# Preparing an expert's weight sums: adding transfers in place of GpSimd sums, and signs moved into activations and shares

## The chip, the cores and the metric

The kernel runs on one core of a Trainium2 chip. The metric is the device time of one execution in microseconds. Three executions of the kernel before took 1699.41, 1706.53 and 1699.93 us; their median is 1699.93 us.

The engines are named as in the profile: PE is TensorE with its matmuls (PEld its weight loads), DVE is VectorE, ACT is ScalarE, POOL is GpSimd, and SP is SyncE, which issues nearly all transfers.

## The reference

Three layers follow each other. First an attention (2 batches, 8 heads, 768 positions, 64 wide) in which a query sees only the keys that have the same nearest centroid. Its output, 1536 tokens of 512, goes through a feed-forward layer, and then through 8 experts whose shares come from a balanced gate:

```python
h = x @ w_in                                  # 512 -> 2048
g = np.maximum(h, 0.0) + np.log1p(np.exp(-np.abs(h)))
x = g @ w_out                                 # 2048 -> 512

P = np.exp(x @ w_gate - max)                  # 1536 x 8, then 8 rounds of
                                              # normalizing rows and columns
for e in range(8):
    h = np.maximum(x @ w1[e], 0.0)            # 512 -> 1024
    out += P[:, e:e+1] * (h @ w2[e])          # 1024 -> 512
```

## The kernel before, in words

**The work and its stages.** Everything is float32, and a float32 product is made of three matmuls on a high and a low part of each operand. So each operand is split: ACT makes the high part, DVE or POOL subtracts it from the original for the low part. The attention takes the first 315 us, the feed-forward layer runs from 315 to about 612 us, the experts from 636 us to the end. The expert stage does 16 passes (2 batches times 8 experts), `NB` of them with index `k`; its first layer is `l1_group` (L899 is its matmul), its second `l2_piece` (L934).

**Seven products in place of eight.** Each expert product is cut into 2 x 2 blocks, and both layers use a scheme of seven block products with sums of blocks on both sides (`PROD`). On the side of the activations the sums are S1 to S4 (`SUMS`): A21 + A22, S1 - A11, A11 - A21, A12 - S2. They are made on the fly by `g_sum` (L872, DVE), `x_sums` (L72) and `xc_prep` (L973). On the side of the weights the sums are T1 to T4, which depend on the weights alone: B12 - B11, B22 - T1, B22 - B12 and T2 - B21. Each is needed twice (once for each batch), so they are made once, in advance, and stored to the DRAM tensors `TD`. From there the expert stage loads them like the blocks that need no sum: `w1_load` (L801, L806, L813, L817) into `wf` and `w1r`, and `w2_load` (L849, L851) into `w2r`.

**Making the sums before the change.** A unit of this work is one tile `ts` of 128 x 4 x 256: a piece of each of the four blocks of one weight matrix. `JOBS` lists 64 units, four for each of 16 matrices. `t_load` (L195) loads the pieces with two transfers from SP, `t_sums` (L201) makes the four sums in place with four subtractions on POOL, `t_store` (L206, L211) writes them to `TD` from SP:

```python
b11, b12, b21, b22 = (t[:, n, :] for n in range(4))
for o_, u_, v_ in ((b11, b12, b11), (b12, b22, b12), (b22, b22, b11), (b21, b21, b22)):
    nc.gpsimd.tensor_tensor(o_, u_, v_, ALU.subtract)
```

Sixteen units (two experts' matrices) are planned into the attention, 24 into the feed-forward layer, 24 into the expert stage. Tiles `ts` have 3, 4 and 1 buffers in the three stages.

**What sets the order.** The attention is a list of events with a step each (`at`), written out in that order. The feed-forward layer goes over 16 blocks of work (`m1`), each with seven places `i`; `tsum_at` puts the sums' parts at such places, a new unit every 3.9 of them. The expert stage is a list of calls with a time (`do`), sorted by it; a time unit is one group of first-layer products, a pass has `G1` = 28 of them, and a new unit of sums comes every 7. The time of a call is its place in the program; the order on each engine and each queue is then made by a scheduler that may put an instruction forward where its operands allow it. On the chip each engine and each queue works strictly in its order, so an instruction that waits holds up whatever is behind it.

**What else is on POOL.** In the feed-forward layer POOL makes low parts of the weights (L243, L247) and of x (L100). In the expert stage it makes the low parts of the second layer's weights, vl (L857), and of a part of the first layer's, wlCm (L829). In the attention it splits q, k and v (L355, L356, L49, L372) and does parts of the choice of centroids (L416, L424). The feed-forward layer's weights are 64-bit words, which DVE turns into float32 (`to32`, L118 to L121) ahead of the splits; its activation ends on DVE with gf (L660), whose low part is L663.

Of the kernel before, what the change touches and what calls it, by code (L numbers as in the profile page):

```python
# [7 lines left out]
F32 = mybir.dt.float32  # L8
# [3 lines left out]
AF = mybir.ActivationFunctionType  # L12
# [8 lines left out]
def attention_moe_moe2(ctx, tc, v, qt, kt, centroids, w_in, w_out, w_gate, w1, w2, eye, out, dbg=None):  # L21
# [39 lines left out]
    def x_blocks(x):  # L61
# [1 line left out]
        return {f"A{i + 1}{j + 1}": x[:, j * hk : (j + 1) * hk, i * h2 : (i + 1) * h2] for i in range(2) for j in range(2)}  # L63

    SUMS = {
        "S1": ("A21", "A22", ALU.add), "S2": ("S1", "A11", ALU.subtract),
        "S3": ("A11", "A21", ALU.subtract), "S4": ("A12", "S2", ALU.subtract),
    }

    def x_sum(blk, name, t, eng):  # L70
        u, v, op = SUMS[name]
        eng.tensor_tensor(t, blk[u], blk[v], op)  # L72
        blk[name] = t

    def x_sums(key, x):
# [103 lines left out]
        [tc.dram_tile([4, NF2, P, DM // 2], F32, name=f"td1_{e}") for e in range(E)],  # L179
    ]  # L180
    TS = {}
    TORD = ("T1", "T3", "T4", "T2")

    def t_load(pool, m, e, u):
        t = TS[m, e, u] = slot_pool[pool].tile([P, 4, 256], F32, tag="ts", name=f"ts{m}_{e}_{u}", bufs=TSB[pool])
        for h in range(2):
            if m:
                o = h * HF + u * P
                src, d = w2[e, o : o + P, :].rearrange("p (s d) -> p s d", s=2), t[:, 2 * h : 2 * h + 2, :]
            else:  # L190
                k, c = divmod(u, 2)
                o = h * DM // 2 + k * P
                src = w1[e, o : o + P, :].rearrange("p (s f) -> p s f", s=2)[:, :, c * 256 : (c + 1) * 256]
                d = t[:, 2 * h : 2 * h + 2, :]
            nc.sync.dma_start(d, src)  # L195

    def t_sums(m, e, u):
        t = TS[m, e, u]
        b11, b12, b21, b22 = (t[:, n, :] for n in range(4))
        for o_, u_, v_ in ((b11, b12, b11), (b12, b22, b12), (b22, b22, b11), (b21, b21, b22)):  # L200
            nc.gpsimd.tensor_tensor(o_, u_, v_, ALU.subtract)  # L201

    def t_store(m, e, u):
        t = TS.pop((m, e, u))
        if m:
            nc.sync.dma_start(TD[1][e][:, u].rearrange("s p d -> p s d"), t)  # L206
            return
        k, c = divmod(u, 2)
        cs = slice(c * 256, (c + 1) * 256)
        for n, ts_ in enumerate((t[:, 0:4:3, :], t[:, 1:3, :])):  # L210
            nc.sync.dma_start(TD[0][e][2 * n : 2 * n + 2, k, :, cs].rearrange("s p f -> p s f"), ts_)  # L211

    TSB = {"ap": 3, "fp": 4, "gp": 1}
    JOBS = [(m, e, u) for e in range(E) for m in range(2) for u in range(NF2)]
    JA, JF = 4 * NF2, 10 * NF2

    WT = {}

# [103 lines left out]
    def at(step, fn, cat=None):  # L322
        events.append((step, len(events), fn, cat))
# [266 lines left out]
        at(92 + (n - 1) * 1.36, lambda n=n: fetch_first(n), ("fu", 0))  # L590
    for n in range(4):
        at(175 + n * 5, lambda n=n: x_split("1_0", first_blk, n), ("xs", 0))
    for n, job in enumerate(JOBS[:JA]):
        t = 22 + 10 * n
        for o, fn, c_ in ((0, t_load, "tl"), (8, t_sums, "tq"), (17, t_store, "tw")):
            at(t + o, lambda fn=fn, job=job: fn(*((("ap",) if fn is t_load else ()) + job)), (c_, 0))
    KEEP = {'sp2': 1, 'fr': 0, 'av': 1, 'am3': 1, 'tpa': 1, 'smc': 0, 'm0': 1, 'rw': 1, 'pz': 1, 'e1': 1}
    events.sort(key=lambda x: x[:2])
    last_prep = max(key for key, _, fn, _ in events if fn in prep_fns)
# [100 lines left out]
    nc.gpsimd.memset(ones_f, 1.0)  # L700
    lt = mp.tile([P, B * NT, E], F32, tag="lt", name="lt", bufs=1)
    Pt = mp.tile([P, B * NT, E], F32, tag="Pt", name="Pt", bufs=1)

    def gtile(shape, tag, b, nm):
        return ps_y.tile(shape, F32, tag=tag, name=nm) if b else ps_l.tile(shape, F32, tag="lb", name=nm)
# [33 lines left out]
    def sinkhorn(it, ph):  # L739
        n = B * NT  # L740
        if ph == 0:
            rs = mp.tile([P, n], F32, tag="rs", name=f"rs{it}", bufs=1)
            nc.vector.tensor_reduce(rs, Pt, AX.X, ALU.add)
            nc.vector.tensor_scalar(rs, rs, 1e-9, None, ALU.add)
            nc.vector.reciprocal(rs, rs)
            nc.vector.tensor_tensor(Pt, Pt, rs.unsqueeze(2).to_broadcast([P, n, E]), ALU.mult)
            cs = G["cs"] = mp.tile([P, E], F32, tag="cs2", name=f"cs{it}", bufs=1)
            nc.vector.tensor_reduce(cs, Pt.rearrange("p t e -> p e t"), AX.X, ALU.add)
            return
        cs = G["cs"]  # L750
        cp = ps_y.tile([P, E], F32, tag=f"y{2 + it % 2}", name=f"cp{it}")
        nc.tensor.matmul(cp, ones_f, cs, start=True, stop=True)
        nc.vector.tensor_scalar(cs, cp, 1e-9, float(E) / N, ALU.add, ALU.mult)
        nc.vector.reciprocal(cs, cs)
        nc.vector.tensor_tensor(Pt, Pt, cs.unsqueeze(1).to_broadcast([P, n, E]), ALU.mult)

    def run(*steps):
        for l in steps:
# [105 lines left out]
        return t  # L864

    def g_sum(k, name, p):
        u_, v_, op = SUMS[name]
        if name in ("S1", "S2"):
            t = x_tile(k, name, p)
        else:  # L870
            t = XG[k, name, p] = XG[k, {"S3": "A21", "S4": "A12"}[name], p]
        nc.vector.tensor_tensor(t, XG[k, u_, p], XG[k, v_, p], op)  # L872

    def g_split(k, i, p):
        src = XG[k, PROD[i][0], p]
# [7 lines left out]
    def l1_group(k, u, i):  # L883
# [33 lines left out]
            else:  # L917
                nc.vector.tensor_tensor(t[:, v], ps, LB["c", {1: 0, 4: 3, 5: 2}[i]], ALU.add)  # L918
        if v and i != 6:
            nc.scalar.activation(t, t, AF.Relu)  # L920

    def l2_piece(k, i, p, t):
        sb, e = divmod(k, E)
# [19 lines left out]
        for t_ in ((0, 1) if t == 1 else (2,)):  # L943
            m = r * HT + t_
            src = y[t_ // 2][:, t_ % 2 * 256 : t_ % 2 * 256 + 256]
            acc = yv[:, m, c * 256 : (c + 1) * 256]
            scl = Pt[:, sb * NT + m, e : e + 1]
            with tc.high_priority(30):
                if e == 0 and i in (0, 2, 3, 6):
                    nc.vector.tensor_scalar(acc, src, scl, None, ALU.mult)  # L950
                else:
                    nc.vector.scalar_tensor_tensor(acc, src, scl, acc, ALU.mult, ALU.add)  # L952
            if e == E - 1 and i in (5, 6):
                nc.sync.dma_start(out.rearrange("(b p t) d -> b t p d", b=B, t=NT)[sb, m], yv[:, m])

    def xc_prep(sb, step):
# [7 lines left out]
            ]  # L964

        def add(name):
            a, b, op = SUMS[name]
            if name == "S4":
                t = blk["S2"]
            else:  # L970
                tag = {"S1": "A22", "S2": "A12", "S3": "A21"}[name]
                t = gp.tile([P, 2, FH], F32, tag="X" + tag, name=f"x{name}{key}", bufs=XB[tag])
            nc.vector.tensor_tensor(t, blk[a], blk[b], op)  # L973
            blk[name] = t

        def split(name):
# [17 lines left out]
    for k in range(NB):  # L994
# [26 lines left out]
        for j in range(14):  # L1021
# [2 lines left out]
            do(first[j] + 0.1, g_split, k, i, p)  # L1024
            for n in range(3):
                do(S0 + lag + sp * j + sp * n / 3 + 0.01, l2_piece, k, i, p, n)
    for n, job in enumerate(JOBS[JF:]):
        t = G1 + 7 * n + 1.5
        do(t, t_load, "gp", *job)
        do(t + 3, t_sums, *job)  # L1030
        do(t + 5.5, t_store, *job)
    for hf in range(2):
        do(0.5 + hf, lambda hf=hf: gate(1, hf))
        do(2.5 + 1.5 * hf, lambda hf=hf: gate_max(hf))
# [2 lines left out]
            do(5.5 + 4 * it + 2.5 * ph, lambda it=it, ph=ph: sinkhorn(it, ph))  # L1037

    tsum_at = {}
    for n, job in enumerate(JOBS[JA:JF]):  # L1040
        for o, fn in ((0, lambda job=job: t_load("fp", *job)), (5, lambda job=job: t_sums(*job)),
                      (10, lambda job=job: t_store(*job))):
            tsum_at.setdefault(divmod(int(3.9 * n) + o, 7), []).append(fn)

    for n, u in enumerate(m1):
        if dbg is not None and n == dbg.get("cut"):
# [75 lines left out]
```

## Time and profile before

| | us |
|---|---|
| median of three executions | 1699.93 |
| the profiled execution | 1703.77 |
| its span, from the first to the last instruction | 1702.0 |
| PE busy | 1552.5 (91%) |
| DVE busy | 1277.2 (75%) |
| ACT busy | 1007.3 (59%) |
| POOL busy | 852.2 (50%) |
| POOL busy with the weights' sums (L201, 256 instructions) | 228.0 |

The page gives an average over stages that have different limits. To read it, one goes from the slices to the windows: a stretch in which PE runs its matmuls back to back at a granted clock of 1.00 gives the rate of that stage, and the stretches that fall short of it are those where something can be gained or lost.

### The profile page before, as it was taken

What the parts mean: (1) busy time and instruction counts of PE and PEld (TensorE: products, weight loads), DVE (VectorE), ACT (ScalarE), POOL (GpSimd) and SP (SyncE); (2) the same over time, 40 slices, a digit from 0 to 9 for tenths busy, and PEclk for the clock granted to TensorE, in tenths of its full rate; (3) what the DMA queues carried; (4) which work ended last, traced back from release to release, by engine and by line L of the source; (5) the groups of instructions that cost most, each with busy time, mean ns of one, the idle gap of its engine ahead of it and who ended that gap; (6) DMA issues with size and microseconds to landing.
All of it is one profiled execution on the core that took longest, in us unless ns stands there. A gap on an engine that the chain in (4) does not pass through costs nothing. (4 is left out here: it accounts for less than half of the span.)

```text
span 1702.0 us, 27339 instructions
## 1 busy us (share of the span) xinstructions
PE 1552.5 (91%) x9873; PEld 1474.4 (87%) x9873; DVE 1277.2 (75%) x1835; ACT 1007.3 (59%) x1854; POOL 852.2 (50%) x728
## 2 busy tenths in 40 slices
PE   5898888798799998888788999998999999999998
PEld 4787877687799977887778999998999999999998
DVE  4988878896666366966565788789788787878877
ACT  4777777654465544554454665665565666656664
POOL 3443545676611125666666454456445455444554
PEclk7998999899999999999998999999999999999999
DMA  7657663467622005555555444433443444334422
GB/s 217 175 157 193 173 176 120 131 229 248 209 75 75 22 26 164 177 183 167 179 178 173 127 121 119 127 117 94 148 129 119 127 124 124 114 115 125 122 78 75
DMA packets 265464, 236.27 MB, mean 139 GB/s; under 512 B 13296, under 2 KB 244848, under 8 KB 265328
## 3 DMA queue, kind: packets, MB, share of 16 engines
q1 hardware_dynamic: 265184, 234.46, 45.6%
q8 instruction: 77, 1.26, 0.3%
q14 instruction: 59, 0.48, 0.1%
q10 hardware_dynamic: 144, 0.07, 0.0%
HBM read 177.32 MB, written 36.70 MB: 126 GB/s over the span
## 5 line engine op out<-in xcount | busy, mean ns | idle before, releaser
L857 POOL TENSOR_TENSOR vl<-w2r,vh 128x512 fp32r<-128x512 f32 x224 | 354.3, 1584 | 373.4 <-ACT vh L856 339.6
L201 POOL TENSOR_TENSOR ts<-ts 128x256 f32<-128x256 f32 x256 | 228.0, 894 | 123.5 <-DMA ts<-in_moe_w_dram 109.7
L878 DVE TENSOR_TENSOR gl<-XA,gh 128x768 fp32r<-128x768 f32 x160 | 172.9, 1082 | 86.7 <-ACT gh L877 86.5
L877 ACT CAST gh<-XA 128x768 fp32r<-128x768 f32 x160 | 133.9, 837 | 148.5 <-PE Ya1m L934 134.8
L934 PE MATMUL Ya0m<-vl,gh 128*128 128x256 f32 x512 | 145.9, 285 | 0.0
L934 PE MATMUL Ya0m<-vh,gl 128*128 128x256 f32 x512 | 145.9, 285 | 0.0
L934 PE MATMUL Ya0m<-vh,gh 128*128 128x256 f32 x512 | 145.9, 285 | 0.0
L856 ACT CAST vh<-w2r 128x512 fp32r<-128x512 f32 x224 | 137.6, 615 | 11.0 <-PE y L680 8.2
L536 DVE TENSOR_TENSOR el<-t,eh 128x384 fp32r<-128x384 f32 x192 | 102.6, 549 | 21.8 <-ACT eh L532 20.3
L934 PE MATMUL Yb0m<-vl,gh 128*128 128x256 f32 x384 | 109.4, 285 | 4.0 <-POOL vl L857 4.0
L934 PE MATMUL Yb0m<-vh,gl 128*128 128x256 f32 x384 | 109.6, 285 | 2.1 <-DVE gl L878 2.1
L934 PE MATMUL Yb0m<-vh,gh 128*128 128x256 f32 x384 | 109.3, 285 | 2.3 <-DVE x L952 2.3
L497 DVE TENSOR_REDUCE sc<-s 128x1 f32<-128x768 f32 x96 | 91.1, 950 | 25.9 <-PE s L489 25.6
L532 ACT CAST eh<-t 128x384 fp32r<-128x384 f32 x192 | 91.1, 481 | 29.0 <-PE t L529 19.5
L529 PE MATMUL t<-idf,E 128*128 128x128 f32 x576 | 100.3, 284 | 5.3 <-ACT OHT L437 2.8
L920 ACT ACTIVATE XA<-XA 128x768 f32<-128x768 f32 x96 | 81.1, 845 | 34.5 <-DVE XA L918 34.5
L502 ACT ACTIVATE E<-s,sc 128x768 f32<-128x768 f32 x96 | 87.1, 907 | 20.4 <-DVE sc L497 19.3
L934 PEld LDWEIGHTS Ya0m<-vh,gl 128*128 128x128 f32 x512 | 98.9, 193 | 0.0
L934 PEld LDWEIGHTS Ya0m<-vh,gh 128*128 128x128 f32 x512 | 98.9, 193 | 0.0
L934 PEld LDWEIGHTS Ya0m<-vl,gh 128*128 128x128 f32 x512 | 98.8, 193 | 0.0
L529 PEld LDWEIGHTS t<-idf,E 128*128 128x128 f32 x576 | 75.0, 146 | 16.0 <-DVE el L536 5.2
L877 ACT CAST gh<-XS 128x768 fp32r<-128x768 f32 x64 | 53.4, 836 | 58.4 <-PE Yb1m L934 44.2
(243 smaller groups left out, 5355.0 us busy)
## 6 DMA issues: line engine op xcount, KB each, us to landing
ts<-in_moe_w_dram SPq DMA_DIRECT2D x128, 256.0 KB, 4.0
w2r<-td SPq DMA_DIRECT2D x64, 512.0 KB, 4.0
w2r<-in_moe_w_dram SPq DMA_DIRECT2D x48, 512.0 KB, 3.6
td<-ts SPq DMA_DIRECT2D x64, 256.0 KB, 3.7
td<-ts SPq DMA_DIRECT2D x32, 512.0 KB, 3.3
wf<-td SPq DMA_DIRECT2D x64, 256.0 KB, 3.1
w1r<-td SPq DMA_DIRECT2D x64, 256.0 KB, 3.1
AT<-HL SPq DMA_DIRECT2D x64, 192.0 KB, 3.9
```

Source lines behind the costliest of these rows:

```text
L201: nc.gpsimd.tensor_tensor(o_, u_, v_, ALU.subtract)
L497: nc.vector.tensor_reduce(SC[i][:, 0, j, t : t + 1], Et[i, t][:, :, 0:CB], AX.XY, ALU.max, negate=True)
L502: nc.scalar.activation(e.rearrange("p (a c) -> p a c", a=2), Et[i, t][:, :, 0:CB], AF.Exp, bias=sc[:, 0, j, t : t + 1], scale=1.0, accum_o ...
L529: nc.tensor.transpose(pt[:, t * P : (t + 1) * P], Et[i, t][:, s * P : (s + 1) * P], idf)
L532: nc.scalar.copy(eh, TT[i, s])
L536: nc.vector.tensor_tensor(el, TT.pop((i, s)), EHL[i, s].bitcast(F32), ALU.subtract)
L856: nc.scalar.copy(h, src)
L857: nc.gpsimd.tensor_tensor(l, src, h.bitcast(F32), ALU.subtract)
L877: nc.scalar.copy(h, src)
L878: nc.vector.tensor_tensor(l, src, h.bitcast(F32), ALU.subtract)
L920: nc.scalar.activation(t, t, AF.Relu)
L934: nc.tensor.matmul(ps, g[:, v, ts], w[:, v, :], start=i in (0, 1, 3) and p == 0 and v == 0 and n == 0 and t != 1, stop=p == 1 and v == 1 a ...
```

## The change

Each weight matrix is now one chain of ten steps on one tile of 128 x 1024, a whole block at a time. Three kinds of steps: a plain load of a block (SP), a load that adds a block to what the tile holds (issued by POOL, `accum_op=ALU.add`), and a store of the tile to `TD` (SP). `STEPS` lists them: load B11, add B12, store T1, add B22, store T2, add B21, store T4, load B12, add B22, store T3. There are 16 chains in place of 64 units: 4 in the attention, 6 in the feed-forward layer, 6 in the expert stage, with 1, 2 and 1 tiles. Each step is bound behind the last PE instruction written before it (`behind_pe`), which holds it at its place in the schedule; it adds no wait on the chip. The steps come 4.1 steps apart in the attention, 2.85 places apart in the feed-forward layer (two chains side by side) and 2.75 time units apart in the expert stage.

So that all of these sums are additions, some blocks and sums change their sign. On the activations' side S1 = A22 - A21, S2 = -S1 - A11, S3 = A11 - A21 and S4 = -S2 - A12, of which S2 and S4 become scalar_tensor_tensor instructions. The first layer's activations take Relu with a scale of -1 where the block comes out negated (all but A11 and A21), and the second layer's right half is added with `Nt`, the negated shares, in place of `Pt`.

```diff
     SUMS = {
-        "S1": ("A21", "A22", ALU.add), "S2": ("S1", "A11", ALU.subtract),
-        "S3": ("A11", "A21", ALU.subtract), "S4": ("A12", "S2", ALU.subtract),
+        "S1": ("A22", "A21", 1.0, ALU.subtract), "S2": ("S1", "A11", -1.0, ALU.subtract),
+        "S3": ("A11", "A21", 1.0, ALU.subtract), "S4": ("S2", "A12", -1.0, ALU.subtract),
     }
+    def sum_op(eng, out_, a, b, sign, op):
+        if sign > 0:
+            eng.tensor_tensor(out_, a, b, op)
+        else:
+            eng.scalar_tensor_tensor(out_, a, sign, b, ALU.mult, op)
...
-    TORD = ("T1", "T3", "T4", "T2")
...
+    TORD = ("T1", "T2", "T3", "T4")
+    STEPS = ("B11", "+B12", "T1", "+B22", "T2", "+B21", "T4", "B12", "+B22", "T3")
+
+    def t_step(pool, m, e, n):
+        what = STEPS[n]
+        if n == 0:
+            TS[m, e] = slot_pool[pool].tile([P, 1024], F32, tag="ts", name=f"ts{m}_{e}", bufs=TSB[pool])
+        t, w = TS[m, e], what.lstrip("+")
+        t = t.rearrange("p (k f) -> p k f", k=NF2 if m else 2)
+        if w[0] == "T":
+            nc.sync.dma_start(TD[m][e][TORD.index(w)].rearrange("k p f -> p k f"), t)
+            return
...
+        src = src.rearrange("(k p) f -> p k f", p=P)
+        if what[0] == "+":
+            nc.gpsimd.dma_start(t, src, accum_op=ALU.add)
+        else:
+            nc.sync.dma_start(t, src)
+
+    def behind_pe(fn, *args):
+        traced = nc.cur_bb.bb.instructions
+        ref, last = next(iter(last_of_engines(("PE",)))), traced[-1]
+        fn(*args)
+        start = next(n for n in reversed(range(len(traced))) if traced[n] is last) + 1
+        for ins in list(traced[start:]):
+            tc.add_manual_dep(
+                ins, ref.name,
+                mybir.DependencyInfo(mybir.DependencyClass.NoSync, mybir.DependencyReason.DATA), reason="order",
+            )
...
-    TSB = {"ap": 3, "fp": 4, "gp": 1}
-    JOBS = [(m, e, u) for e in range(E) for m in range(2) for u in range(NF2)]
-    JA, JF = 4 * NF2, 10 * NF2
+    TSB = {"ap": 1, "fp": 2, "gp": 1}
+    JOBS = [(m, e) for e in range(E) for m in range(2)]
+    JA, JF = 4, 10
...
-    for n, job in enumerate(JOBS[:JA]):
-        t = 22 + 10 * n
-        for o, fn, c_ in ((0, t_load, "tl"), (8, t_sums, "tq"), (17, t_store, "tw")):
-            at(t + o, lambda fn=fn, job=job: fn(*((("ap",) if fn is t_load else ()) + job)), (c_, 0))
+    for j, job in enumerate(JOBS[:JA]):
+        for n in range(10):
+            at(22 + 42 * j + 4.1 * n, lambda job=job, n=n: behind_pe(t_step, "ap", *job, n), ("tl", 0))
...
+        if it == 7:
+            nc.vector.tensor_scalar(Nt, Pt, -1.0, None, ALU.mult)
...
-            nc.scalar.activation(t, t, AF.Relu)
+            nc.scalar.activation(t, t, AF.Relu, scale=1.0 if name == "A11" else -1.0)
...
-            scl = Pt[:, sb * NT + m, e : e + 1]
+            scl = (Nt if c else Pt)[:, sb * NT + m, e : e + 1]
...
-    for n, job in enumerate(JOBS[JF:]):
-        t = G1 + 7 * n + 1.5
-        do(t, t_load, "gp", *job)
-        do(t + 3, t_sums, *job)
-        do(t + 5.5, t_store, *job)
+    for j, job in enumerate(JOBS[JF:]):
+        for n in range(10):
+            do(G1 * (j + 1) - 22 + 2.75 * n, behind_pe, t_step, "gp", *job, n)
...
-    for n, job in enumerate(JOBS[JA:JF]):
-        for o, fn in ((0, lambda job=job: t_load("fp", *job)), (5, lambda job=job: t_sums(*job)),
-                      (10, lambda job=job: t_store(*job))):
-            tsum_at.setdefault(divmod(int(3.9 * n) + o, 7), []).append(fn)
+    for j, job in enumerate(JOBS[JA:JF]):
+        for n in range(10):
+            tsum_at.setdefault(divmod(1 + int(14.5 * (j // 2 * 2) + 10 * (j % 2) + 2.85 * n), 7), []).append(
+                lambda job=job, n=n: behind_pe(t_step, "fp", *job, n)
+            )
```

## Rows read from the trace of the kernel before

**Rows 1.** the page's 40 slices: busy tenths of PE

```profile
PE   5898888798799998888788999998999999999998
```

**Rows 2.** windows: PE, PEld, DVE, ACT, POOL busy us (x); PEclk, DMA share, GB/s

```profile
340.00:468.00 128.00, 108.19 (x565) 99.11 (x564) 94.13 (x128) 64.84 (x129) 90.58 (x96) 0.93 0.70 229
468.00:540.00 72.00, 72.00 (x417) 67.63 (x416) 48.50 (x82) 44.35 (x86) 12.35 (x9) 1.00 0.20 65
...
700.00:920.00 220.00, 179.06 (x1151) 174.07 (x1150) 136.29 (x180) 102.69 (x173) 150.26 (x130) 0.92 0.58 177
...
1000.00:1100.00 100.00, 100.00 (x696) 99.02 (x695) 77.53 (x103) 63.67 (x109) 49.50 (x34) 1.00 0.41 125
```

**Rows 3.** windows of the instructions on tile ts alone

```profile
0.00:315.00 315.00, 50.03 (x64) 0.91 0.59 164
...
340.00:468.00 128.00, 73.30 (x82) 0.93 0.70 229
468.00:540.00 72.00, 0.00 (x0) 1.00 0.20 65
...
700.00:920.00 220.00, 72.97 (x76) 0.92 0.58 177
```

**Rows 4.** waits of PE, 700 to 920 us: us in total, times, longest us

```profile
PE l0m L899 <- POOL wlCm L829: 35.4, 9, 4.8
```

**Rows 5.** waits of PE, 340 to 468 us

```profile
PE p L646 <- DVE gf L660: 19.7, 8, 4.4
```

**Rows 6.** lines of POOL, 700 to 920 us: busy, mean ns; idle before, releaser

```profile
L201 POOL TENSOR_TENSOR ts<-ts 128x256 f32<-128x256 f32 x76 | 73.4, 966 | 71.0 <-DMA ts<-in_moe_w_dram 65.9 <-issue 1.8
L857 POOL TENSOR_TENSOR vl<-w2r,vh 128x512 fp32r<-128x512 f32 x39 | 59.5, 1534 | 1.6 <-ACT vh L856 1.6
```

**Rows 7.** lines of POOL, 1000 to 1100 us

```profile
L857 POOL TENSOR_TENSOR vl<-w2r,vh 128x512 fp32r<-128x512 f32 x23 | 36.3, 1578 | 47.9 <-ACT vh L856 46.3 <-DMA w1r<-in_moe_w_dram 1.6
```

**Rows 8.** lines of DVE, 340 to 468 us

```profile
L663 DVE TENSOR_TENSOR gl<-gf,gh 128x384 fp32r<-128x384 f32 x25 | 21.1, 844 | 5.9 <-ACT gh L662 5.9
...
L118 DVE TENSOR_SCALAR cm<-cm 128x512 f32<-128x512 f32 x17 | 12.1, 714 | 2.6 <-ACT cm L117 2.6
L120 DVE SCALAR_TENSOR_TENSOR w2f<-r,w2f 128x512 int32<-128x512 int32 x8 | 9.4, 1173 | 0.2
```

**Rows 9.** lines of DVE, 468 to 612 us

```profile
L663 DVE TENSOR_TENSOR gl<-gf,gh 128x384 fp32r<-128x384 f32 x33 | 23.1, 701 | 13.7 <-ACT gh L662 13.7
...
L120 DVE SCALAR_TENSOR_TENSOR w2f<-r,w2f 128x512 int32<-128x512 int32 x5 | 3.5, 693 | 0.2
...
L118 DVE TENSOR_SCALAR cm<-cm 128x512 f32<-128x512 f32 x8 | 3.4, 424 | 0.1
```

**Rows 10.** the stores of line 206: duration ns min/median/max, first and last start

```profile
L206 SPq DMA_DIRECT2D td<-ts x32: 360/377/1552, 137.5 to 919.2; - x32
```

**Rows 11.** DMA issues (KB each, median us to landing), and landings of tile ts

```profile
ts<-in_moe_w_dram SPq DMA_DIRECT2D x128, 256.0 KB, 4.0
w2r<-td SPq DMA_DIRECT2D x64, 512.0 KB, 4.0
...
td<-ts SPq DMA_DIRECT2D x64, 256.0 KB, 3.7
td<-ts SPq DMA_DIRECT2D x32, 512.0 KB, 3.3
...
DMA to landing us min/median/max: 2.1/3.9/7.8
```

**Rows 12.** waits of PE, 0 to 315 us

```profile
PE po L431 <- POOL OH L424: 13.7, 5, 3.4
```

**Rows 13.** lines of DVE, whole span, shapes apart

```profile
L352 DVE SCALAR_TENSOR_TENSOR HL<-rT,HL 128x768 fp32r<-128x768 f32 x2 | 1.9, 956 | 0.3 <-ACT HL L347 0.3
...
L72 DVE TENSOR_TENSOR xS<-xS,x 128x768 f32<-128x768 f32 x1 | 0.9, 944 | 0.0
```

**Rows 14.** waits of SP's queue, 640 to 920 us

```profile
SPq L195 <- DMA td<-ts: 40.6, 20, 4.6
```

More of the change, by code (lines that the diff above doesn't have):

```diff
@@ L65, in attention_moe_moe2 @@
     SUMS = {
-        "S1": ("A21", "A22", ALU.add), "S2": ("S1", "A11", ALU.subtract),
-        "S3": ("A11", "A21", ALU.subtract), "S4": ("A12", "S2", ALU.subtract),
-    }
+        "S1": ("A22", "A21", 1.0, ALU.subtract), "S2": ("S1", "A11", -1.0, ALU.subtract),
+        "S3": ("A11", "A21", 1.0, ALU.subtract), "S4": ("S2", "A12", -1.0, ALU.subtract),
+    }
+    def sum_op(eng, out_, a, b, sign, op):
[3 more added lines that the diff above has]
+            eng.scalar_tensor_tensor(out_, a, sign, b, ALU.mult, op)
     def x_sum(blk, name, t, eng):
-        u, v, op = SUMS[name]
-        eng.tensor_tensor(t, blk[u], blk[v], op)
+        u, v, sign, op = SUMS[name]
+        sum_op(eng, t, blk[u], blk[v], sign, op)
         blk[name] = t
@@ L181, in attention_moe_moe2 @@
     TS = {}
-    TORD = ("T1", "T3", "T4", "T2")
[L184 to L204, printed above, removed]
-        if m:
[L206 to L211, printed above, removed]
@@ L213, in attention_moe_moe2 @@
-    TSB = {"ap": 3, "fp": 4, "gp": 1}
-    JOBS = [(m, e, u) for e in range(E) for m in range(2) for u in range(NF2)]
-    JA, JF = 4 * NF2, 10 * NF2
+    TORD = ("T1", "T2", "T3", "T4")
[9 more added lines that the diff above has]
+            return
+        a, b = int(w[1]) - 1, int(w[2]) - 1
+        if m:
+            src = w2[e, a * HF : (a + 1) * HF, b * DM // 2 : (b + 1) * DM // 2]
+        else:
+            src = w1[e, a * DM // 2 : (a + 1) * DM // 2, b * HF : (b + 1) * HF]
+        src = src.rearrange("(k p) f -> p k f", p=P)
+        if what[0] == "+":
+            nc.gpsimd.dma_start(t, src, accum_op=ALU.add)
+        else:
+            nc.sync.dma_start(t, src)
@@ L702, in attention_moe_moe2 @@
     Pt = mp.tile([P, B * NT, E], F32, tag="Pt", name="Pt", bufs=1)
+    Nt = mp.tile([P, B * NT, E], F32, tag="Nt", name="Nt", bufs=1)
     def gtile(shape, tag, b, nm):
@@ L866, in g_sum @@
     def g_sum(k, name, p):
-        u_, v_, op = SUMS[name]
+        u_, v_, sign, op = SUMS[name]
         if name in ("S1", "S2"):
@@ L871, in g_sum @@
             t = XG[k, name, p] = XG[k, {"S3": "A21", "S4": "A12"}[name], p]
-        nc.vector.tensor_tensor(t, XG[k, u_, p], XG[k, v_, p], op)
+        sum_op(nc.vector, t, XG[k, u_, p], XG[k, v_, p], sign, op)
     def g_split(k, i, p):
@@ L966, in add @@
         def add(name):
-            a, b, op = SUMS[name]
+            a, b, sign, op = SUMS[name]
             if name == "S4":
@@ L972, in add @@
                 t = gp.tile([P, 2, FH], F32, tag="X" + tag, name=f"x{name}{key}", bufs=XB[tag])
-            nc.vector.tensor_tensor(t, blk[a], blk[b], op)
+            sum_op(nc.vector, t, blk[a], blk[b], sign, op)
             blk[name] = t
```

## The prediction

> **What bounds the kernel now.** I read the page first: its line of 40 slices for PE shows two stretches that are mostly under 9, the first eleven slices and the 16th to the 22nd; after those PE is nearly full [rows 1]. Then the table of windows, which turns this into lost time. In 468 to 540 us PE runs 417 matmuls in 72 us with a granted clock of 1.00, 5.79 per us, and in 1000 to 1100 us it runs 696, 6.96 per us [rows 2]. These are the rates of the two stages (feed-forward and experts) when nothing holds PE up. In 340 to 468 us it runs 565, which are 565/5.79 = 97.6 us of work: 30.4 us are lost, 19.8 of them with PE idle (128 - 108.2) and the rest at a clock of 0.93. In 700 to 920 us it runs 1151, 165.4 us of work: 54.6 us are lost, 40.9 idle (220 - 179.1), the rest at a clock of 0.92 [rows 2]. The clock is lower just where PE waits, so whoever removes the wait gets both back.
>
> Both stretches are those in which GpSimd sums the weights' blocks. The windows of tile ts put 73.3 and 73.0 us of sums there, and none into the two stretches at full rate [rows 3]. By the program's times the units of the expert stage come 7 time units apart; a time unit is one group of PE's work there, about 2.16 us (1.07 + 1.07 of products as the matmul rate gives them: 6 + 9 matmuls at 6.96 per us). That would be 15 us apart; 76 sums, 19 units, in 220 us are 11.6 us apart [rows 3]. So the old units run ahead of their place and crowd; the same holds for the 24 units of the feed-forward stage, which are planned over 14 of 16 blocks and are all done by 468 us.
>
> Who waits: in 700 to 920 us PE waits 35.4 us for POOL's wlCm, which is nearly all of its idle time [rows 4]; in 340 to 468 us it waits 19.7 us for DVE's gf (L660) [rows 5]. POOL itself, in 700 to 920 us, spends 73.4 us on sums and 71.0 us waiting for the loads of their operands, and next to nothing waiting for ACT [rows 6]; in 1000 to 1100 us it waits 46 us for ACT, which is its slack [rows 7]. POOL is thus the bound in the first half of the expert stage: per unit of four sums it gives away (73.4 + 71.0)/19 = 7.6 us, 30.4 us per weight matrix of four units. In the feed-forward stage the bound is DVE, and its instructions are longer there than in 468 to 612 us, for the same shapes: L118 714 against 424 ns, L663 844 against 701, L120 1173 against 693 [rows 8, 9].
>
> **The change part by part.**
>
> *Sums off GpSimd, expert stage.* Six matrices are prepared there. Removed: 16 sums and their load waits per matrix, 30.4 us of POOL. Added: 4 transfers that POOL issues, each behind the landing of the step before it. What one costs POOL is not in the trace, since POOL issues no transfer. From below it is the 0.38 us that SP's L206 takes to issue [rows 10]; from above, POOL arrives when the step before has just been issued and stands for its landing, about 4.0 us for w2r<-td [rows 11], so 4.4. The steps are placed 2.75 time units, 5.9 us, apart, longer than that landing, so the lower end is nearer; I take 2.0 (the longest issue of L206, 1.55, and a little wait). Then a matrix costs POOL 8 us in place of 30.4. POOL is busy 49.5 of 100 us at full rate [rows 2]; 8 us more per 28 time units (60 us) leave it slack. PE's wait for POOL is 35.4 of 40.9 us idle [rows 2, 4], and with its share of the clock 54.6 x 35.4/40.9 = 47.3 us. If that shrinks as POOL's time does (to 8/30.4), 35 us come back; if all lost time goes, 54.6. I take the middle, **45 us**.
>
> *The landing of an adding transfer.* It reads its target too. From below it lands like a plain one of 512 KB, 3.3 to 4.0 us [rows 11], from above like two after each other, 8 us. I take 6. Store, next addition: an addition may take 2 x 5.9 - 3.3 = 8.5 us before POOL has to stand for the store behind it, so this fits, and SP, which stores one step after it, would hardly stand. What is queued behind on SP are the loads of w1r, wf and w2r; they wait for POOL and DVE to free buffers anyway. The Trainium skill (DMA: Bandwidth & Descriptors, section "Anatomy of one DMA — SWDGE (gpsimd) path") gives about 2.0 us plus bytes/436e3 for a transfer issued by GpSimd, which would be an estimated 3.2 us here; no row shows one, and by it the gain would be the upper end, 1633 in all.
>
> *Feed-forward stage.* POOL's 73.5 us of sums go and 24 issues come, spread over 14 blocks instead of the first third. DVE's excess in the rows compared is 17 x 0.29 + 25 x 0.143 + 8 x 0.48 = 12.3 us [rows 8, 9]. It is on PE's path through gf. From below 5 us, since 17 of L118's conversions fall into this stretch and 8 into the longer one after it, and that crowd stays; from above all 30.4. I take **12 us**, the excess, for it is what the sums on POOL are seen to cost DVE.
>
> *Attention.* 50 us of sums go [rows 3] and 16 issues come. PE's largest wait for POOL there is 13.7 us, for OH [rows 12]. If the sums were the reason, 14 come back; if POOL stands behind a late step of SP as often, 14 are lost. I take 0.
>
> *More bytes, fewer issues.* Per matrix two plain loads, four stores and four additions of 512 KB, against 2 MB in and 2 MB out before: B12 and B22 are read twice, 1 MB more. SP's issues for these fall from 224 (128 + 64 + 32 [rows 11]) to 96. The transfers hide beside PE as now: the queues are busy 0.58 in 700 to 920 us [rows 2], and the steps are spread wider. 0; if that cover went, it would show in the landing above.
>
> *Signs.* S2 and S4 become scalar_tensor_tensor: 956 against 944 ns for 128x768 [rows 13], 64 of them, 0.8 us of DVE, which is busy 78 of 100 us at full rate: 0. A scale in Relu and Nt in place of Pt are other operands of the same instructions, 0; forming Nt is one small DVE instruction behind the gate: 0.
>
> Sum: 45 + 12 = 57 us. The profiled execution took 1703.8 us with a span of 1702.0; the median of the runs is 1699.9, 3.8 below. 57 off the median: **1643 us**.
>
> **The rivals.**
>
> *The wait takes the place of the sums.* Each of POOL's issues stands for the landing before it, 4.4 us: 17.6 us per matrix. The expert stage then gives 47.3 x (1 - 17.6/30.4) = 20, the feed-forward stage, for the same waits, not 12 but its lower end and a little, 8: 1672. For it: POOL already waits 71 us for loads, and SP, on which those loads stand, waits 40.6 us for ts to be stored [rows 6, 14]. Against it: the spacing of 5.9 us.
>
> *DVE holds POOL's issues up.* DVE's and POOL's instructions lengthen each other now [rows 8, 9]. If an issue waits out a DVE instruction of about 1.2 us (L120's length there), POOL pays 3.2 us per addition, 12.8 per matrix, and the stage gives 47.3 x (1 - 12.8/30.4) = 27: 1661 with the 12. The Trainium skill (SBUF — State Buffer, "SBUF: two separate sides") says that descriptors of a GpSimd transfer can't be written while VectorE runs a two-port instruction; so far no row shows such a transfer.
>
> *Slower: additions are dear.* The place is POOL's queue. It decides from 7.6 us of POOL per addition: 4 x 7.6 are the 30.4 that the sums cost now. At 12 us a matrix costs 48, PE's loss per matrix of 47.3/4.75 = 10.0 us (19 units are 4.75 matrices) grows to 15.7, 35 us over six matrices, and in attention 192 us of POOL against 50 [rows 3] cost about the lower end above, 14: 1749. For it: the cost of 512 rows' worth of transfer on POOL is unknown, and each of these issues sits ahead of vl and wlCm. Against it: transfers of these tiles land within 7.8 us at the longest [rows 11], so only the issuing itself could be that long.
>
> *It does nothing.* The lost time has another cause (conversions on DVE in one stretch, transfers in the other), 1692 to 1708. Against it: the full rate sets in where the sums end, twice.
>
> **How the numbers follow.** Forecast 0.50, wait in place of sums 0.16, DVE holding up 0.08, dear additions 0.16, nothing 0.10. A measurement here can tell about 0.5%, 8.5 us, from no change. Faster: 0.50 + 0.16 + 0.08 = 0.74; same 0.10; slower 0.16. The forecast's own range is 1615 (54.6 + 30.4) to 1660 (35 + 5); for 8 in 10 it takes in the two smaller gains and most of no change: 1615 to 1702.
>
> **What would show it.** Right: 1000 to 1100's matmul rate already at 700 to 900 us; PE's wait for wlCm below 10 us there; POOL waiting for ACT in that stretch; L118 near 424 ns at 340 to 468 us; POOL's transfers near 2 us. Wrong: a long POOL time per transfer, POOL waiting for td<-ts or ts with vl behind it, an attention stage that ends after 315 us, or a loss that stays in both stretches with POOL idle.

## The result, and the profile after

The changed kernel takes 1625.98 us (median of four runs, 1623.11 to 1627.69) against 1701.0 us before in the same measurement. The ratio is 0.9552, with a 95% interval of 0.9525 to 0.9578: it is 4.5% faster, 75 us. The prediction was 1643 us, 57 us faster, in a range of 1615 to 1702.

The span of the profiled execution falls from 1702.0 to 1624.9 us. The slices of PE and of POOL on the page after:

```profile
PE   5888889989999999899999999998999999999998
...
POOL 3333333432323122355555555555455454445544
```

The first of the two stretches that were under 9 [rows 1] now ends with the sixth slice, but for the ninth, and of the second, slices 16 to 22 before, only slice 17 is left. POOL is at 4 or less up to slice 17.

The first matmul of each stage (of the feed-forward groups, of the first expert's first layer) divides the spans. This table is used below for every kernel; the ends are read from the matmuls of those two lines.

| kernel | attention | feed-forward | experts | span |
|---|---|---|---|---|
| before | 315.2 | 321.2 | 1065.6 | 1702.0 |
| after | 317.6 | 295.7 | 1011.6 | 1624.9 |

So 54.0 us come from the experts and 25.5 us from the feed-forward stage, and attention is 2.4 us longer. The windows of the changed kernel, with the columns of [rows 2]:

```profile
340.00:468.00 128.00, 124.52 (x710) 115.83 (x710) 91.50 (x156) 78.21 (x153) 38.22 (x30) 1.00 0.86 220
468.00:540.00 72.00, 70.79 (x405) 65.98 (x405) 40.96 (x69) 42.20 (x83) 22.77 (x17) 1.00 0.84 213
676.00:920.00 244.00, 237.06 (x1640) 233.34 (x1639) 199.39 (x245) 146.49 (x247) 133.15 (x94) 0.98 0.76 203
...
1000.00:1100.00 100.00, 98.28 (x697) 96.92 (x696) 85.71 (x106) 66.33 (x112) 54.44 (x33) 1.00 0.36 112
```

In 340 to 468 us PE runs 710 matmuls where it ran 565 [rows 2], 97.6 us of work before and 710/5.79 = 122.6 us now. The window from 676 us starts as far behind the start of the expert stage (63 us) as that from 700 us did before. PE runs 1640 matmuls in its 244 us: 1640/6.96 = 235.6 us of work, 8.4 us lost, where 54.6 were lost in 220 us [rows 2]. The granted clock is 0.98 in place of 0.92. PE's longest waits in that stretch are no longer for POOL, which took 35.4 us [rows 4]:

```profile
PE l3m L910 <- DVE XA L929: 4.0, 3, 2.6
PE l0m L910 <- ACT XA L927: 2.7, 1, 2.7
```

POOL's lines in 600 to 1100 us, first the row of the sums before, then the changed kernel:

```profile
L201 POOL TENSOR_TENSOR ts<-ts 128x256 f32<-128x256 f32 x96 | 91.7, 955 | 96.0 <-DMA ts<-in_moe_w_dram 90.2 <-issue 1.8
```

```profile
L868 POOL TENSOR_TENSOR vl<-w2r,vh 128x512 fp32r<-128x512 f32 x101 | 162.3, 1615 | 176.6 <-ACT vh L867 175.9 <-DMA w1r<-in_moe_w_dram 0.7
...
L207 POOL DMA_DIRECT2D ts<-in_moe_w_dram x24 | 30.0, 1250 | 41.6 <-DMA td<-ts 21.3 <-DMA ts<-in_moe_w_dram 11.1 <-PE cp L761 9.2
```

Before, the 96 sums of this stage took POOL 91.7 us, and it stood another 96.0 us ahead of them: 187.7 us for six matrices, 31.3 us each, about the 30.4 that the prediction had from the shorter stretch of [rows 6]. Now 24 adding transfers cost 30.0 + 41.6 = 71.6 us, 11.9 us per matrix, and POOL waits for ACT instead (175.9 us ahead of vl), which is its slack.

The feed-forward stage's DVE rows, as in [rows 8]:

```profile
L671 DVE TENSOR_TENSOR gl<-gf,gh 128x384 fp32r<-128x384 f32 x29 | 18.2, 629 | 8.3 <-ACT gh L670 8.3
...
L126 DVE SCALAR_TENSOR_TENSOR w2f<-r,w2f 128x512 int32<-128x512 int32 x10 | 11.0, 1097 | 0.3
L124 DVE TENSOR_SCALAR cm<-cm 128x512 f32<-128x512 f32 x20 | 9.7, 483 | 3.0 <-ACT cm L123 2.9
```

L118 is now L124 and down from 714 to 483 ns, L663 (now L671) from 844 to 629, L120 (now L126) hardly, 1173 to 1097. Whether that is the reason for the 25.5 us is taken up below.

### The profile page after: what moved, and what is told of

It is laid out like the page before. It is cut to its first block, busy times and chain, and to the rows that moved or that the text cites. A ratio compares the mean times of both kernels' runs of the same rounds, so it can differ in the third digit from the quotient of the medians.

```text
span 1624.9 us, 26977 instructions
## 1 busy us (share of the span) xinstructions
PE 1527.6 (94%) x9873; PEld 1449.9 (89%) x9873; DVE 1257.0 (77%) x1836; ACT 1005.4 (62%) x1854; POOL 706.5 (43%) x536
## 3 DMA queue, kind: packets, MB, share of 16 engines
q0 software_dynamic: 25600, 33.56, 13.3%
## 5 line engine op out<-in xcount | busy, mean ns | idle before, releaser
L868 POOL TENSOR_TENSOR vl<-w2r,vh 128x512 fp32r<-128x512 f32 x224 | 359.2, 1608 | 410.7 <-ACT vh L867 402.3
L889 DVE TENSOR_TENSOR gl<-XA,gh 128x768 fp32r<-128x768 f32 x160 | 180.2, 1126 | 79.0 <-ACT gh L888 79.0
L207 POOL DMA_DIRECT2D ts<-in_moe_w_dram x64 | 80.8, 1270 | 193.0 <-DMA ts<-in_moe_w_dram 74.0
L538 PE MATMUL t<-idf,E 128*128 128x128 f32 x576 | 100.6, 284 | 11.9 <-DVE el L545 9.9
L538 PEld LDWEIGHTS t<-idf,E 128*128 128x128 f32 x576 | 74.8, 146 | 23.7 <-DVE el L545 13.4
L72 DVE TENSOR_TENSOR XS<-XA,XA 128x768 f32<-128x768 f32 x32 | 62.4, 1949 | 33.4 <-ACT XA L927 33.4
```

Source lines behind the costliest of these rows:

```text
L538: nc.tensor.transpose(pt[:, t * P : (t + 1) * P], Et[i, t][:, s * P : (s + 1) * P], idf)
L868: nc.gpsimd.tensor_tensor(l, src, h.bitcast(F32), ALU.subtract)
L889: nc.vector.tensor_tensor(l, src, h.bitcast(F32), ALU.subtract)
```

## The experiments

Two theories stood against each other. The first is the prediction's: an adding transfer takes POOL less time than four sums and the wait for their loads, and DVE is not lengthened any more. The second is that the operation matters little, and that what counts is the place: `behind_pe` keeps the steps from running ahead and crowding. The change does both at once, so the first two runs do one without the other.

**Old sums, bound behind PE.** The edit to the kernel before, in each of the three stages:

```diff
-        do(t, t_load, "gp", *job)
-        do(t + 3, t_sums, *job)
-        do(t + 5.5, t_store, *job)
+        do(t, behind_pe, t_load, "gp", *job)
+        do(t + 3, behind_pe, t_sums, *job)
+        do(t + 5.5, behind_pe, t_store, *job)
```

> The kernel before, with only the binding behind PE added to its loads, sums and stores; the sums stay on GpSimd. If POOL's time is what mattered (my theory), a unit still costs POOL 4 sums (3.9 us) plus some waiting; spread from 11.6 to 15 us apart, POOL is still nearly full in the expert stage, so only about half of the 54 us there comes back, and the feed-forward stage, whose DVE still meets the sums, returns under 10 of its 25: about 1665. If the crowding alone was the fault (rival), the binding returns nearly all: about 1630.

Measured: 1633.08 us, ratio 0.9592 (0.9571 to 0.9613). The rival is right about the whole: the binding alone, with every sum still on GpSimd, returns 4.1 of the 4.5%.

**Adding transfers, not bound.** The edit to the changed kernel, in `behind_pe`:

```diff
         fn(*args)
+        return
```

> The changed kernel without the binding behind PE, so that the adding chains may run ahead of their place. If taking the sums off POOL is what counts, most of the gain stays: 1630 to 1645, with POOL waiting more for landings than the 142 us of the changed kernel. If the place is what counts, the chains crowd like the old units, POOL stands behind each landing, and the time is back near 1690.

Measured: 1712.98 us, ratio 1.0051 (1.0034 to 1.0068). It is half a per cent slower than the kernel before, and slower too than the 1690 us that I gave the rival, because the feed-forward stage is 13.5 us longer than before. The adding transfers by themselves gain nothing.

**Signs only.** The kernel before with `SUMS`, `sum_op`, the scaled Relu and the negated shares of the change; the shares lie in the tile of the gate's logits, which is free by then. On the side of the weights:

```diff
-            nc.gpsimd.tensor_tensor(o_, u_, v_, ALU.subtract)
+            nc.gpsimd.tensor_tensor(o_, u_, v_, ALU.add)
...
+    Nt = lt
```

> The kernel before with the signs alone moved: the sums of weights are additions on GpSimd, S2 and S4 are scalar_tensor_tensor, Relu has a scale, the negated shares are used. My theory: nothing, 1697 to 1705. Rival: the signs carry part of the 2.4 us lost in attention or cost DVE in the expert stage, then 5 us or more slower.

Measured: 1701.56 us, ratio 0.9991 (0.9975 to 1.0006). Nothing, as expected.

**No preparing at all.** The edit to the changed kernel; the loads of T3, T4 and of the second layer's sums are turned in the same way.

```diff
-    JA, JF = 4, 10
+    JA, JF = 0, 0
+    JOBS = []
...
-                TD[0][e][0:2, :, :, u * P : (u + 1) * P].rearrange("s k p f -> p (s k) f"),
+                w1[e, :, u * P : (u + 1) * P].rearrange("(k p) f -> p k f", p=P),
```

> The changed kernel without any preparing of weight sums: no chains, and the loads of T1 to T4 take blocks of the weights of the same size instead; so the sums of weights are left out. This is the floor. My theory: the adding chains cost PE almost nothing in the last two stages, so the floor is 1615 to 1623, and what is left of loss at 640 to 700 us and after 1100 us stays. Rival: chains still cost through SP or shared transfers, then the floor is below 1605.

Measured: 1583.06 us, ratio 0.929. The rival's time is right: preparing the sums still costs the changed kernel 43 us. By stage it is 25.3 us of attention, 6.0 of the feed-forward stage and 11.9 of the experts. Whether SP or shared transfers are the reason, as the rival had it, this run can't tell; the run with plain transfers below gives 28.6 of the 43 us to the adding itself. The stages of these four kernels:

| kernel | attention | feed-forward | experts | span |
|---|---|---|---|---|
| old sums, bound | 304.9 | 295.1 | 1031.7 | 1631.7 |
| adding, not bound | 312.7 | 334.7 | 1063.8 | 1711.2 |
| signs only | 316.0 | 321.1 | 1065.6 | 1702.7 |
| no preparing | 292.3 | 289.7 | 999.7 | 1581.7 |

What the binding does shows in the rows. In the expert stage, POOL's row of the old sums when bound, and of the adding transfers when not:

```profile
L201 POOL TENSOR_TENSOR ts<-ts 128x256 f32<-128x256 f32 x96 | 91.4, 952 | 40.5 <-DMA ts<-in_moe_w_dram 32.0 <-issue 2.2 <-POOL vl L868 0.9
```

```profile
L207 POOL DMA_DIRECT2D ts<-in_moe_w_dram x24 | 30.0, 1251 | 158.0 <-DMA ts<-in_moe_w_dram 81.1 <-DMA td<-ts 54.7 <-PE l1m L911 10.9
```

Bound, the old sums take the same 91 us, but POOL stands 40.5 us ahead of them in place of 96.0. Not bound, the adding transfers take 30.0 us, but POOL stands 158.0 us ahead of them: 188.0 us in all, as much as the sums before (187.7). In the feed-forward stage, DVE's waits for POOL, 315 to 600 us, in the kernel before, the changed one, with bound sums, and with unbound adding:

```profile
DVE wf L119 <- POOL wlBD L243: 11.5, 4, 7.3
...
DVE w2f L119 <- POOL w2l L247: 5.8, 2, 3.5
```

```profile
DVE wf L125 <- POOL wlBD L252: 3.9, 4, 3.1
```

```profile
DVE wf L119 <- POOL wlBD L254: 1.1, 4, 0.4
```

```profile
DVE w2f L125 <- POOL w2l L257: 27.4, 3, 11.4
...
DVE wf L125 <- POOL wlBD L253: 12.4, 4, 8.0
```

PE's waits in this stage, 317 to 600 us, in the same four kernels:

```profile
PE p L646 <- DVE gf L660: 23.1, 9, 4.4
PE p L646 <- POOL clA L100: 6.1, 1, 6.1
```

```profile
PE p L654 <- DVE gf L668: 9.9, 7, 2.9
```

```profile
PE p L657 <- DVE gf L671: 8.7, 6, 3.2
```

```profile
PE p L655 <- DVE gf L669: 35.2, 10, 9.2
```

POOL makes the low parts of the converted weights there, and DVE can't convert the next ones into the same tiles before. When POOL is behind a crowd of sums or behind a landing, DVE stands at its conversion, gf is queued behind it, and PE waits for gf. DVE's waits of 17.3, 3.9, 1.1 and 39.8 us and PE's for gf of 23.1, 9.9, 8.7 and 35.2 us go with stages of 321.2, 295.7, 295.1 and 334.7 us. The length of DVE's instructions does not. These are the lines of [rows 8], in the same window, with bound sums and with unbound adding:

```profile
L674 DVE TENSOR_TENSOR gl<-gf,gh 128x384 fp32r<-128x384 f32 x30 | 22.3, 743 | 9.9 <-ACT gh L673 9.9
L118 DVE TENSOR_SCALAR cm<-cm 128x512 f32<-128x512 f32 x19 | 11.3, 596 | 0.0
L120 DVE SCALAR_TENSOR_TENSOR w2f<-r,w2f 128x512 int32<-128x512 int32 x10 | 9.1, 910 | 0.3
```

```profile
L672 DVE TENSOR_TENSOR gl<-gf,gh 128x384 fp32r<-128x384 f32 x23 | 13.8, 601 | 7.3 <-ACT gh L671 7.3
L126 DVE SCALAR_TENSOR_TENSOR w2f<-r,w2f 128x512 int32<-128x512 int32 x7 | 10.2, 1453 | 0.2
L124 DVE TENSOR_SCALAR cm<-cm 128x512 f32<-128x512 f32 x15 | 6.3, 422 | 6.7 <-ACT cm L123 6.6
```

Summed over these three lines against the lengths of [rows 9], DVE's excess is 12.3 us before, 5.2 after, 6.7 with bound sums and 5.3 with unbound adding (a line that is shorter than there counts as nothing). It falls about alike in three kernels, of which two gain 26 us in this stage and the third loses 13.5. The account by DVE's and PE's waits rests on these four kernels side by side; no run takes away this one wait alone.

A second set asks what about the place it is: the spacing, the place in POOL's queue or that in SP's; and what the adding costs by itself.

**Bound, but crowded.** The first experiment with the expert stage's units closer together:

```diff
-        t = G1 + 7 * n + 1.5
+        t = G1 + 5 * n + 1.5
```

> The first experiment (old sums, all bound) with the expert stage's units 5 time units apart in place of 7, about the 11 us at which the kernel before ran them. If the crowding of POOL's queue is the fault: the expert stage goes from 1031.7 back to 1055 to 1066 us, 1656 to 1667 in all. If the binding helps in another way, by the order on the queues and whatever the spacing: 1630 to 1638.

Measured: 1657.89 us, ratio 0.9726 (0.9693 to 0.976); the expert stage takes 1056.0 us and the other two are as in the first experiment. So most of the binding's gain in this stage is spacing: of the 33.9 us that it brought, 24.3 are gone again. The other 9.6 stay; the units ran 13.5 us apart on average, against 12.0 in the kernel before and 16.4 in the first experiment. POOL stands for loads nearly as long as in the kernel before, and from 600 to 1000 us PE waits for wlCm again:

```profile
L201 POOL TENSOR_TENSOR ts<-ts 128x256 f32<-128x256 f32 x96 | 92.9, 967 | 85.2 <-DMA ts<-in_moe_w_dram 71.9 <-issue 8.1 <-POOL vl L868 0.6
```

```profile
PE l0m L910 <- POOL wlCm L840: 27.9, 9, 6.7
```

**Only the sums bound.** The edit to the first experiment, alike in all three stages:

```diff
-        do(t, behind_pe, t_load, "gp", *job)
+        do(t, t_load, "gp", *job)
         do(t + 3, behind_pe, t_sums, *job)
-        do(t + 5.5, behind_pe, t_store, *job)
+        do(t + 5.5, t_store, *job)
```

> The kernel before with only the four sums of each unit bound behind PE; loads and stores are free to run ahead as buffers allow. If what counts is where the sums stand in POOL's queue (new theory): 1630 to 1640, as with everything bound. If what counts is the place of the transfers in SP's queue: above 1660.

Measured: 1620.85 us, ratio 0.9507 (0.9478 to 0.9535), better than I gave it. The place in POOL's queue is what counts, and free loads are better than bound ones, because they have landed when POOL comes to the sums:

```profile
L201 POOL TENSOR_TENSOR ts<-ts 128x256 f32<-128x256 f32 x96 | 103.5, 1078 | 5.6
```

POOL stands 5.6 us, not 40.5, ahead of the same sums, and the expert stage goes from 1031.7 to 1019.2 us. This kernel has no adding transfer, and can't be told apart from the changed one: the intervals of the two ratios overlap. What is left of PE's waits in this stage is for DVE; none for POOL's wlCm is among them (600 to 1000 us):

```profile
PE l3m L913 <- DVE XA L932: 10.6, 7, 2.7
```

**Only the adding steps bound.** The same for the changed kernel:

```diff
         fn(*args)
+        if STEPS[args[-1]][0] != "+":
+            return
```

> The changed kernel with only the adding steps bound behind PE, plain loads and stores free. If POOL's place is the lever here too: the stages that the full binding wins stay won, 1618 to 1630, against 1713 with nothing bound. If the chain needs SP's steps in place: above 1650.

Measured: 1617.66 us, ratio 0.9499 (0.9468 to 0.953). Binding POOL's steps alone is enough here too. Against the run before it, the old sums with only POOL's part bound, it is 3 us shorter, and their intervals overlap: with either operation held at its place on POOL and the rest free, the two runs show no difference in the whole. By stage, adding is 7.6 us longer in attention and 7.3 us shorter with the experts. POOL's row in 600 to 1100 us:

```profile
L207 POOL DMA_DIRECT2D ts<-in_moe_w_dram x24 | 30.0, 1249 | 31.5 <-DMA td<-ts 18.0 <-DMA ts<-in_moe_w_dram 4.4 <-PE cp L763 3.8
```

**Plain transfers in place of adding ones.**

```diff
-            nc.gpsimd.dma_start(t, src, accum_op=ALU.add)
+            nc.gpsimd.dma_start(t, src)
```

> The changed kernel with the four adding transfers of a chain as plain ones, still issued by POOL; the adding of blocks is left out. If the landing of 7.1 us is due to the adding, it falls to about 4, POOL's 142 us of waiting fall below 70, and attention comes back from 317 to about 305 us: 1608 to 1616. If the issuing on POOL and the added bytes are what costs: 1620 to 1627.

Measured: 1597.43 us, ratio 0.9373 (0.9348 to 0.9399). The gain is larger than I gave either side: the adding itself, with its longer issue, costs 1625.98 - 1597.43 = 28.6 us. POOL's waits for landings did not fall as far as I said, from 141.6 to 89.8 us and not below 70. The queue of POOL's transfers, their landing and their issue, first with adding (the changed kernel), then plain:

```profile
q1 hardware_dynamic: 242656, 217.67, 44.2%
q0 software_dynamic: 25600, 33.56, 13.3%
...
ts<-in_moe_w_dram POOLq DMA_DIRECT2D x64, 512.0 KB, 7.1
td<-ts SPq DMA_DIRECT2D x64, 512.0 KB, 3.6
...
ts<-in_moe_w_dram SPq DMA_DIRECT2D x32, 512.0 KB, 4.8
```

```profile
L207 POOL DMA_DIRECT2D ts<-in_moe_w_dram x64: 1188/1284/1784, 82.6 to 976.7; - x64
```

```profile
q0 software_dynamic: 9216, 33.56, 6.4%
...
ts<-in_moe_w_dram POOLq DMA_DIRECT2D x64, 512.0 KB, 4.9
```

```profile
L207 POOL DMA_DIRECT2D ts<-in_moe_w_dram x64: 704/766/913, 81.6 to 947.1; - x64
```

For the same 33.56 MB the queue takes 13.3% of the 16 engines' span in place of 6.4%, a transfer lands in 7.1 us in place of 4.9, and issuing it holds POOL for 1284 ns (median) in place of 766. All three stages gain: attention 317.6 to 301.7 us, feed-forward 295.7 to 290.8, experts 1011.6 to 1001.7.

**Sums in attention, adding after it.** Attention is where the changed kernel lost against bound sums, 317.6 to 304.9 us. Its POOL waits there, 50 to 300 us, and those with bound sums:

```profile
POOL ts L207 <- DMA ts<-in_moe_w_dram: 26.8, 3, 13.9
...
POOL ts L207 <- DMA td<-ts: 25.4, 4, 9.6
```

```profile
POOL ts L201 <- DMA ts<-in_moe_w_dram: 2.8, 1, 2.8
```

So the four chains of attention go back to 16 bound units of sums, and the other twelve stay:

```diff
-    for j, job in enumerate(JOBS[:JA]):
-        for n in range(10):
-            at(22 + 42 * j + 4.1 * n, lambda job=job, n=n: behind_pe(t_step, "ap", *job, n), ("tl", 0))
+    for n, job in enumerate(UNITS):
+        t = 22 + 10 * n
+        for o, fn, c_ in ((0, t_load, "tl"), (8, t_sums, "tq"), (17, t_store, "tw")):
+            at(t + o, lambda fn=fn, job=job: behind_pe(fn, *((("ap",) if fn is t_load else ()) + job)), (c_, 0))
```

> The changed kernel, but the attention's four matrices are prepared as before, in 16 units with sums on GpSimd (as additions), bound behind PE as in the first experiment. Stage by stage the earlier runs give 304.9 us (attention, bound sums) + 295.7 (feed-forward, adding) + 1011.6 (experts, adding) = 1612.2 of span, about 1614. If the stages are independent: 1610 to 1618, faster than both. If the attention's 12.7 us between bound sums and adding chains is not due to the adding transfers: about 1626.

Measured: 1612.77 us, ratio 0.9462 (0.9431 to 0.9494). The stages are independent, as far as this run can tell: 304.0, 295.8 and 1010.3 us, each within 1.3 us of what the earlier runs gave.

**The same, with attention's loads and stores free.**

```diff
-            at(t + o, lambda fn=fn, job=job: behind_pe(fn, *((("ap",) if fn is t_load else ()) + job)), (c_, 0))
+            if fn is t_sums:
+                at(t + o, lambda fn=fn, job=job: behind_pe(fn, *job), (c_, 0))
+            else:
+                at(t + o, lambda fn=fn, job=job: fn(*((("ap",) if fn is t_load else ()) + job)), (c_, 0))
```

> The fifth experiment (sums on GpSimd in attention, adding chains after it), with only the sums of the attention's units bound behind PE and their loads and stores free. Stage by stage: 300.4 (attention with only the sums bound) + 295.8 + 1010.3 = 1606.5 of span, about 1608, if POOL standing for loads is what is left of it in attention; 1613 as before if not.

Measured: 1609.21 us, ratio 0.9448 (0.941 to 0.9486), the fastest of the kernels that compute the whole reference, about 17 us under the changed one. It can't be told apart from the one before it, and its attention took 305.1 us, not the 300.4 expected: the step I gave for it did not show. What moves attention by 5 us between kernels whose POOL never stands for its sums stays open.

| kernel | attention | feed-forward | experts | span |
|---|---|---|---|---|
| sums bound, 5 units apart | 305.7 | 294.4 | 1056.0 | 1656.1 |
| only sums bound | 300.4 | 295.0 | 1019.2 | 1614.6 |
| only adding steps bound | 308.0 | 295.3 | 1011.9 | 1615.2 |
| plain transfers | 301.7 | 290.8 | 1001.7 | 1594.2 |
| sums in attention | 304.0 | 295.8 | 1010.3 | 1610.1 |
| the same, loads free | 305.1 | 294.7 | 1009.0 | 1608.8 |

## Why the prediction was right, and where it was not

**The quantity was the right one for the expert stage, as far as PE waits for POOL.** The prediction made PE's loss depend on what one matrix costs POOL, work and standing together. Put in the order of that time for all six matrices (busy plus idle before, from POOL's rows in 600 to 1100 us), the kernels are nearly in the order of their expert stages, whatever the operation:

| kernel | POOL's time, us | expert stage, us |
|---|---|---|
| adding, not bound | 188.0 | 1063.8 |
| before | 187.7 | 1065.6 |
| sums bound, 5 units apart | 178.1 | 1056.0 |
| sums bound | 131.9 | 1031.7 |
| only sums bound | 109.1 | 1019.2 |
| sums in attention | 85.4 | 1010.3 |
| the same, loads free | 78.1 | 1009.0 |
| after | 71.6 | 1011.6 |
| only adding steps bound | 61.5 | 1011.9 |
| plain transfers | 39.6 | 1001.7 |
| no preparing | 0 | 999.7 |

From 188 down to 85 us the stage shortens by some 54; from there to 61 nothing more comes, and the last ten come where the adding goes. PE waits long for wlCm in the first three rows alone (27.8, 40.4 and 27.9 us between 600 and 1000 us). With the sums bound that wait is gone, and what PE waits for there is DVE's XA. So the wait is shown for the upper part of the table; why the stage still shortens by 20 us from 131.9 to 71.6 was not tried.

The term of 45 us was too low, first of all in its scale. The 54.6 us were lost in a window that holds 19 of the 24 units [rows 3], and the sum took them for all six matrices; its rival of dear additions did divide by 4.75. Scaled by 24/19, the bounds of 35 and 54.6 become 44 and 69, and their middle 57, near the 54.0 that the stage gave. No preparing at all gives 65.9. The lower bound, by which PE's loss shrinks as POOL's time does, was too low besides: the loss fell to 11.9/65.9 = 0.18, where POOL's time went to 71.6/187.7 = 0.38. The threshold of the rival of dear additions held: at 7.6 us per addition the gain was to be gone, and unbound the additions cost 188.0/24 = 7.8 us, and in this stage it is gone.

**The step that failed is "Added: 4 transfers ... I take 2.0".** I charged the gain to the operation, with the spacing of 5.9 us as a given. The price of an addition, 71.6/24 = 3.0 us, is half again what I took; and it is what the place makes it, 3.0 bound and 7.8 not. And the same place makes the old sums cheap too. The text saw that the old units "run ahead of their place and crowd", and gave the binding no term of its own. The binding brings 4.1 of the 4.5% with the old sums. The adding costs 0.5% without it, and on top of it 7 us are left (1633.08 to 1625.98); the two intervals overlap, so that this is not shown to be more than noise. By stage it wins 20.1 us with the experts and loses 12.7 in attention. So it is in part luck that 1643 came near 1626: the sum paid the operation for what the place did, its first two terms were too low and attention's too high.

Why the units crowd can be read from the rows ahead, though no run shows it by itself: with one tile in the expert stage, a load of 4.0 us, four sums of 966 ns and a store of 3.3 to 3.7 us are 11.2 to 11.6 us [rows 6, 11], the distance at which they ran. They went round as fast as the tile allowed, and POOL stood for a load in each round.

**The feed-forward term was half its size and had, in the main, the wrong cause.** Forecast 12 us from shorter DVE instructions; measured 25.5. DVE's excess in the lines of the forecast fell by 7.1 us, and as far in the unbound adding, where the stage is the slowest. What goes with the stage is DVE's standing for POOL's splits, 13.4 us less, and with it PE's wait for gf, 13.2 us less. The row that named it, DVE's wait for wlBD and w2l, is not among those on which the prediction rests; it took a difference of durations for the cause because that was of a fitting size.

**Attention** was to be 0 and is 2.4 us longer. By way of the bound sums these are two terms that nearly cancel: with bound sums it is 10.3 us shorter, with adding transfers 12.7 us longer than that. But the binding does not do there what it does in the other stages: unbound adding takes 312.7 us in attention, all steps bound 317.6, the adding steps alone bound 308.0. Why is open. The bounds of 14 both ways held.

**More bytes** were costed at 0. The plain transfers move the same bytes and come within 15 us of no preparing, which is the most that bytes and issues can cost; the adding costs 28.6 us. I put its landing at 6 us; it is 7.1. **Signs**, 0: the ratio of that run is 0.9991, no change.

Two readings were loose. The time unit of 2.16 us is 15/6.96, of which 6 matmuls take 0.86 us and 9 take 1.29, not 1.07 each. And that DVE's and POOL's instructions lengthen each other is in [rows 8, 9] for DVE alone.

The Trainium skill (DMA: Bandwidth & Descriptors, "Anatomy of one DMA — SWDGE (gpsimd) path") led to an estimate of 3.2 us for such a transfer; the trace has 7.1 with adding and 4.9 without, beside this kernel's other traffic, so the measurement decides against it here. The rule of the Trainium skill (SBUF — State Buffer, "SBUF: two separate sides"), by which descriptors wait for VectorE, does not show in the length of the issues: the 64 issues take 1188 to 1784 ns. POOL's 3.0 us per addition are near the 3.2 of that rival, but 1.25 of them are the issue and the rest is standing, by the trace mostly for landings.

Of the signs of being right, PE's matmul rate (6.72 per us from 676 to 920 us), the wait for wlCm and POOL's slack came out; the time per addition was 3.0 us and not near 2. L124 came four fifths of the way, from 714 to 483 ns with 424 as the mark, and meant less than I thought. Of the signs of being wrong two showed as well: attention ends at 317.6 us, and POOL stands for td<-ts (21.3 us) and ts (11.1 us) in the expert stage, without harm to PE there.

## To carry to other kernels

Before an operation is replaced because its engine is full, split that engine's time into work and standing, and ask whether the same work in another place of its queue would stand less; here binding the old sums to their place gave nine tenths of the gain, and the new operation without it gave a loss. Work that runs in advance on an engine that also serves the critical path should be tried with its place on that engine held back to where it is needed, and its loads left free to run ahead; with the old sums the free loads and stores were worth another 12 us here, in attention alone they showed nothing. When a change does two things, run each alone before crediting either.

## What the runs showed of the hardware that I had not expected

A transfer that adds into its target takes about twice the time of the 16 DMA engines that a plain one takes, 13.3% against 6.4% of the span for 33.56 MB, in 25600 against 9216 packets, and lands in 7.1 against 4.9 us. It also takes POOL longer to issue, 1284 against 766 ns. SP issues the plain loads of the same chains (L209 of the changed kernel) in 382 ns (median).

Not settled: in some places POOL's wait ahead of an adding transfer ends with an instruction of DVE or PE on which it does not depend by the program; which wait that is was not tried.
